# Which PSUM ring the small transposes of an attention kernel draw their banks from

## The chip, the cores and the metric

The kernel runs on one core of a Trainium2 chip. The metric is the device time of one execution in microseconds (us). The core's engines work side by side: PE (TensorE) multiplies and transposes matrices, DVE (VectorE), ACT (ScalarE) and POOL (GpSimd) work on elements, and queues, among them SP's (SyncE), issue DMAs. PEld in the profile is PE's loading of a stationary operand, which overlaps its matmuls. PE writes its results to PSUM, which this kernel uses as eight banks of 128 x 512 fp32; ACT and DVE read them from there.

## The reference

Three stages follow one another. The change lies in the first, an attention in which neighbouring pairs of queries are averaged:

```python
q_pool = q.reshape(B, H, S // factor, factor, D).mean(axis=3)
scores = scale * np.matmul(q_pool, k.transpose(0, 1, 3, 2))
scores = scores - np.max(scores, axis=-1, keepdims=True)
attn = np.exp(scores)
attn = attn / (np.sum(attn, axis=-1, keepdims=True) + 1e-09)
return np.matmul(attn, v).astype(np.float32)
```

There are 2 batches, 8 heads, 1152 keys, 576 pooled queries per batch, head size 64. Its 1152 x 512 output goes through a mixture of eight experts (two per row, 512 to 1024 to 512 with a relu), and then through a product with a 512 x 2048 matrix, `h * cos(h)`, and a product back to 512 columns. All is fp32; the kernel splits operands into a high and a low part in fp32r.

## The kernel before

**Tiles.** The attention takes the heads in four pairs (`hp`, 0 to 3; `hl` is the head in the pair). The pooled queries of both batches lie behind one another, 1152 rows, in nine tiles of 128 rows; tile 4 holds rows of both batches. So there are 72 tiles, numbered n = 18 hp + 9 hl + t. The scores of one tile are 128 x 1152, in three pieces of 384 columns, one PSUM bank each.

**One step.** The loop at line 880 is software-pipelined. In step n, PE makes the scores of tile n + 1 (`s_bank`, `s_part`, line 310) and transposes the exponentials p of tile n (`t_pe`, line 348); DVE takes the maxima of tile n + 1 (`s_max`, lines 324 and 326); ACT copies the transposed p as the high part (`t_hi`, line 361), makes the exponentials of tile n + 1 (`s_exp`, line 333), and copies the third piece of p for POOL (`t_pool`, lines 369 to 372); DVE makes the low part (`t_lo`, line 365). Then PE multiplies by the values (`avq`, line 386), nine products of a high and low part in some steps and six in the tiles 2 to 4 (`NPOP`), four of them ahead of the third transposes. The order on PE in one step is: scores 0 and 1, transposes 0, scores 2, transposes 1, four value products, transposes 2, the other value products, and last, in some steps, one small group.

**The small groups.** There are three kinds, each with a PSUM bank of its own for a short time:

- `q_group` (line 129): three transposes of pooled queries of the next head pair (line 136), then two ACT copies (line 140).
- `k_group` (line 174): three transposes of keys of the next head pair (line 180), then one ACT copy (line 181). Each of the two batches' key sets of a head pair takes three.
- `x_group` (line 684): for a row group of two or three tiles whose two heads are done, the products with an identity and the gate's weights (line 694), then two DVE multiplications by 1/sum (lines 706 and 723). In head pair 3, row group 1, ACT copies the bank first (line 698).

`plan()` (line 728) puts the first two kinds into fixed steps; the third goes into the next steps without one of these. In step 70, the last of the loop, the product of head pair 3, row group 1 is issued ahead of all transposes of p.

**PSUM.** The eight banks are three rings of one pool. Each name is a ring whose banks are handed out in turn, and a matmul into a bank waits until the readers of its last contents are done:

```python
def tbank():
    if tail:
        return ps.tile([128, 512], F32, name="s", bufs=4)
    return ps.tile([128, 512], F32, name="pt", bufs=3)
```

`s`, four banks, is for scores; `pt`, three banks, for the transposes of p and, through `tbank()`, for all small groups until the attention's tail; `pa`, one bank, for the value products. Three scores, three transposes and at most one small group are allocated in a step.

The order on every engine is the order of the code; nothing is rearranged. Behind the attention come routing, the experts and the last products (from line 949 on), whose weights DMAs load as buffers come free.

Of the kernel before, what the change touches and what calls it, by code (L numbers as in the profile page):

```python
# [9 lines left out]
F32 = mybir.dt.float32  # L10
# [12 lines left out]
def attn_moe_cos_kernel(ctx, tc, q, k, v, w_gate, w_noise, noise, w1, w2, w_in, w_out, out):  # L23
# [5 lines left out]
    HP = H // 2  # L29
# [35 lines left out]
    ps = pse.enter_context(tc.tile_pool(name="attps", bufs=1, space=PSUM))  # L65
# [56 lines left out]
# [4 lines that stand above are left out]
# [3 lines left out]
    def q_group(hp, j):  # L129
        if j == 0:  # L130
            QS[hp] = prep.tile([128, 1216], F32, name="st", bufs=1)
            nc.gpsimd.memset(QS[hp][:, SQ:QB1], 0.0)
        QR = QS[hp]
        p = tbank()
        for i in range(3):
            nc.tensor.transpose(p[:, i * 128:(i + 1) * 128], QP[hp][:, 3 * j + i].rearrange("p h d -> p (h d)"), ident)
        pv = p[:, 0:384].rearrange("p (i b s) -> p b s i", i=3, b=2)
        for b in range(B):
            o = QR[:, b * QB1:b * QB1 + SQ].rearrange("p (s c) -> p s c", c=9)[:, :, 3 * j:3 * j + 3]
            nc.scalar.activation(o, pv[:, b], AF.Copy, scale=1.0 / 16.0)  # L140
# [33 lines left out]
    def k_group(hp, b, j):  # L174
        if j == 0:
            KS[hp, b] = prep.tile([128, 1216], F32, name="st", bufs=1)[:, 0:S]
        p = tbank()
        for i in range(3):
            c = 128 * (3 * j + i)
            nc.tensor.transpose(p[:, i * 128:(i + 1) * 128], KN[hp, b].rearrange("p h s -> p (h s)")[:, c:c + 128], ident)  # L180
        nc.scalar.activation(KS[hp, b][:, 384 * j:384 * (j + 1)], p[:, 0:384], AF.Copy)
# [213 lines left out]
    def fold_x():  # L395
        hp, hl, g, p, w = fold.pop(0)
        b, lo, hi = GR[g]
        if g == 0:
            XT[hp, hl] = sb.tile([128, N], F32, name="xt", bufs=2)
        if (hp, hl) == (HP - 1, 1) and g > 1:  # L400
            nc.scalar.activation(XT[hp, hl][:, lo:hi], p[:, 0:w], AF.Copy)
        else:
            nc.vector.tensor_copy(XT[hp, hl][:, lo:hi], p[:, 0:w])
        if hl == 1:
            fill.append(lambda mid=None: x_group(hp, g, mid))
# [64 lines left out]
    def logits(hp, ts):  # L470
        acc = LGP[:, ts, 0:2]
        if hp == HP - 1:
            nc.vector.tensor_reduce(LG[:, ts], LGP[:, ts, 0:4].rearrange("p t h e -> p t e h"), axis=AX.X, op=OP.add)
        elif hp:
            nc.gpsimd.tensor_tensor(acc, acc, LGP[:, ts, 2 * hp:2 * hp + 2], op=OP.add)
# [208 lines left out]
    def x_group(hp, g, mid=None):  # L684
        tl = XTL[g]
        nt = len(tl)
        p = tbank()
        for i, t in enumerate(tl):
            if mid and i:
                mid()  # L690
                mid = None
            for hl in range(2):
                c = 160 * i + 80 * hl
                nc.tensor.matmul(p[:, c:c + 80], XT[hp, hl][:, t * 128:(t + 1) * 128],  # L694
                                 GW[:, hp, 16 * hl:16 * hl + 80], start=True, stop=True)
        if (hp, g) == (HP - 1, 1):
            xo = sb.tile([128, 3, 128], F32, name="rw", bufs=2).rearrange("p a b -> p (a b)")
            nc.scalar.activation(xo[:, 0:160 * nt], p[:, 0:160 * nt], AF.Copy)
            p = xo
        pv = p[:, 0:160 * nt].rearrange("p (i k c) -> p i k c", k=10, c=16)  # L700
        hs = slice(2 * hp, 2 * hp + 2)
        ts = slice(tl[0], tl[0] + nt)
        ri = RINV[:, ts, hs]

        def x_logits():
            nc.vector.tensor_tensor(LGP[:, ts, LGS[hp]:LGS[hp] + 2, :],
                                    pv[:, :, 0:10:9],
                                    ri.to_broadcast([128, nt, 2, 16]), op=OP.mult)
            logits(hp, ts)

        x_mul = lambda: x_store(hp, ts, pv[:, :, 1:9].rearrange("p i k c -> p i (k c)"), ri)
        if hp == HP - 1 and g:
            xm.append(x_mul)
            xg.append(x_logits)
        else:
            x_logits()
            x_mul()
# [3 lines left out]
    def x_store(hp, ts, px, ri):  # L721
        xo = X[:, ts, hp * 128:(hp + 1) * 128]
        nc.vector.tensor_tensor(xo.rearrange("p i (h d) -> p i h d", h=2),
                                px.rearrange("p i (h d) -> p i h d", h=2),
                                ri.to_broadcast([128, px.shape[1], 2, 64]), op=OP.mult)
        nc.sync.dma_start(x_d.rearrange("(t p) d -> p t d", p=128)[:, ts, hp * 128:(hp + 1) * 128], xo)

    def plan():
# [5 lines left out]
        for hp in range(HP):  # L734
# [6 lines left out]
            if hp:  # L741
                m = n0 - 18
                if hp > 1:
                    at(m, load_q, hp, 0)
                    at(m + 1, load_q, hp, 1)
                d = 1 if hp == 1 else 0
                at(m + 1 + d, pool_q, hp, 0)
                at(m + 2 + d, pool_q, hp, 1)
                at(m + 2, load_k, hp, 0)
                for j in range(3):  # L750
                    at(m + (3 + 2 * d, 5 + d, 6 + d)[j], q_group, hp, j)
                at(m + 7 + d, q_split, hp)
                at(m + 8 + d, q_asm, hp, 0)
                at(m + 9 + d, q_asm, hp, 1, False)
                for j in range(3):
                    at(m + (8 + d, 9 + d, 10 + d)[j], k_group, hp, 0, j)
                at(m + 11 + d, k_split, hp, 0)
                at(m + 11 + d, load_k, hp, 1)
                at(m + 12 + d, k_asm, hp, 0)
                for j in range(3):  # L760
                    at(m + (14, 15, 16)[j], k_group, hp, 1, j)
                at(m + 17, k_split, hp, 1)
                at(m + 18, k_asm, hp, 1)
                at(n0 + 1, l_asm, hp, 1)
                at(n0 + 1, q_bd, hp, 1)
# [60 lines left out]
    for j in range(3):  # L826
        k_group(0, 1, j)
# [52 lines left out]
    for n in range(NTOT - 1):  # L880
        hp, hl, t = tiles[n]
        for f, a in ev.get(n, []):
            if f not in (q_group, k_group):
                f(*a)
# [53 lines left out]
        if t in GEND:  # L938
            av_push(hp, hl, GEND[t])
            if hl == 1:  # L940
                r_inv(hp, GEND[t])
        fl = [(f, a) for f, a in ev.get(n, []) if f in (q_group, k_group)]
        for f, a in fl:
            f(*a)
# [430 lines left out]
    for e in range(E_N):  # L1375
        last = e == E_N - 1
        for f in range(8):
            s = 8 * e + f
# [334 lines left out]
```

## Time and profile before

| | us |
|---|---|
| median of three runs | 740.85 (740.27 to 741.19) |
| profiled execution | 739.14 |
| its span, first to last instruction | 737.6 |
| PE busy in the span | 722.5 |
| PE's weight loads busy | 673.9 |
| DVE, ACT, POOL busy | 562.3, 528.8, 301.9 |
| attention loop, steps 0 to 70 | about 14 to 270 in the span |

The page gives the busy time of each engine, the chain of work that ended last, and the costliest groups of instructions. "Timeline" lists instructions in order of time; a row may merge neighbours of one kind ("x3" is three of them, and the length is theirs together). "Waits" says who waited for whom; a wait is counted as idle time of the waiting engine. In brackets at the end of a row stands the idle time before it and what ended it. Names such as `s`, `pt` and `p` are the program's tiles: `p<-s,nm` is an exponential that reads the bank s. An ACTIVATE of line 333 is followed by a short read of its sum, which overlaps the next instruction.

### The profile page before, as it was taken

To read this page: it belongs to the slowest core of one execution; us is meant where nothing else is said; L and a number is where in the kernel's file an instruction comes from. 1 tells how busy PE (TensorE), PEld (TensorE's weight loads), DVE (VectorE), ACT (ScalarE), POOL (GpSimd) and SP (SyncE) were. 2 spreads that over 40 slices of the span, in tenths; PEclk is the share of its full clock that TensorE was granted. 3 is DMA by queue.
4 is the path that set the end of the run, shared out by engine and by line. 5 is a ranking of instruction groups with operands and counts; after the bars stand their busy time and mean duration, and the time that the engine had idled before them with its cause. 6 is when DMAs were issued, how large, how long until landed. Compare 5 with 4: busy or idle time off the path is not lost.

```text
span 737.6 us, 13760 instructions
## 1 busy us (share of the span) xinstructions
PE 722.5 (98%) x4803; PEld 673.9 (91%) x4803; DVE 562.3 (76%) x1161; ACT 528.8 (72%) x1200; POOL 301.9 (41%) x329
## 2 busy tenths in 40 slices
PE   6999999999999999999999999999999999999997
PEld 4899999999999989999999999999889989888885
DVE  5888788888878988879889887776677776556562
ACT  5999799979988964458777676766588665555443
POOL 5988867877977973212022021103187110000000
PEclk9999999999999999999999999999999999999999
DMA  9957756695665511798999999968353210010001
GB/s 207 244 94 183 184 130 147 163 237 106 161 140 146 179 44 29 248 314 295 363 371 328 334 345 330 329 233 286 119 171 97 85 29 1 1 44 0 1 1 60
DMA packets 75329, 125.02 MB, mean 169 GB/s; under 512 B 11950, under 2 KB 42030, under 8 KB 75254
## 3 DMA queue, kind: packets, MB, share of 16 engines
q1 hardware_dynamic: 68678, 101.92, 47.3%
q0 software_dynamic: 5568, 19.14, 7.4%
q10 hardware_dynamic: 1008, 3.02, 1.6%
q8 instruction: 40, 0.66, 0.4%
q14 instruction: 35, 0.29, 0.1%
HBM read 82.15 MB, written 20.33 MB: 139 GB/s over the span
## 4 chain that ended last, share of the span: by engine, by line
PE 90%; DVE 4%; ACT 3%; DMA 1%; issue 0%; SPq 0%; ACTq 0%; DVEq 0%
PE h L1145 20%; PE acc L1145 16%; PE acc L1177 11%; PE s L310 10%; PE pa L386 9%; PE pt L348 9%; PE t L1145 7%; PE pt L694 2%; PE t L1137 1%; PE pt L984 1%; PE t L1194 1%; PE pt L180 1%; DMA raw<-in_moe_w_dram 1%; DVE nm L324 1%; DVE el L365 1%; DMA qn<-in_q_dram 1%
## 5 line engine op out<-in xcount | busy, mean ns | idle before, releaser
L324 DVE TENSOR_REDUCE nm<-s 128x1 f32<-128x384 f32 x216 | 112.1, 551 | 23.4 <-PE s L310 21.8
L333 ACT ACTIVATE p<-s,nm 128x384 f32<-128x384 f32 x216 | 125.1, 583 | 2.8 <-DVE nm L326 1.5
L1145 PE MATMUL h<-xe,u 128*128 128x320 f32 (+5 forms) x768 | 120.1, 306 | 0.0
L1145 PEld LDWEIGHTS h<-xe,u 128*128 128x128 f32 x768 | 109.6, 188 | 0.5
L642 DVE TENSOR_TENSOR u<-raw,u 128x1024 fp32r<-128x1024 f32 x66 | 80.9, 1227 | 34.4 <-ACT u L641 33.6
L348 PE MATMUL pt<-ident,p 128*128 128x128 f32 x645 | 105.0, 272 | 0.0
L310 PE MATMUL s<-kt,q 128*128 128x384 f32 x240 | 88.8, 386 | 3.7 <-DVE kt L195 2.1
L348 PEld LDWEIGHTS pt<-ident,p 128*128 128x128 f32 x645 | 81.7, 140 | 5.7
L386 PE MATMUL pa<-eh,v 128*128 128x320 f32 (+1 forms) x279 | 86.5, 324 | 0.0
L641 ACT ACTIVATE u<-raw 128x1024 fp32r<-128x1024 f32 x73 | 77.1, 1057 | 10.3 <-DMA raw<-in_moe_w_dram 5.8
L361 ACT ACTIVATE eh<-pt 128x384 fp32r<-128x384 f32 x144 | 68.9, 501 | 20.3 <-PE pt L348 19.0
L386 PE MATMUL pa<-el,v 128*128 128x320 f32 (+1 forms) x279 | 82.4, 309 | 0.0
L372 POOL TENSOR_TENSOR el<-rw,eh 128x384 fp32r<-128x384 f32 x71 | 71.9, 1012 | 5.9
L365 DVE TENSOR_TENSOR el<-pt,eh 128x384 fp32r<-128x384 f32 x144 | 72.9, 547 | 1.0 <-ACT eh L361 0.9
L1177 PE MATMUL acc<-hh,u 128*128 128x320 f32 (+5 forms) x448 | 71.8, 302 | 0.1
L1145 PE MATMUL acc<-u,gh 128*128 128x512 f32 x216 | 66.9, 391 | 0.0
L310 PE MATMUL s<-kt,l 128*128 128x384 f32 x198 | 66.3, 337 | 0.0
L1177 PEld LDWEIGHTS acc<-hh,u 128*128 128x128 f32 x448 | 64.7, 188 | 0.4 <-ACT hh L1156 0.4
L1232 POOL DMA_DIRECT2D w_d<-dw x16 | 9.0, 563 | 130.5 <-DVE dw L1231 130.5
L371 POOL TENSOR_SCALAR eh<-rw 128x384 fp32r<-128x384 f32 x71 | 36.8, 518 | 42.0 <-ACT rw L369 39.7
L386 PEld LDWEIGHTS pa<-el,v 128*128 128x128 f32 x279 | 52.9, 190 | 0.0
L386 PEld LDWEIGHTS pa<-eh,v 128*128 128x128 f32 x279 | 52.8, 189 | 0.0
(292 smaller groups left out, 1605.9 us busy)
## 6 DMA issues: line engine op xcount, KB each, us to landing
raw<-in_moe_w_dram SPq DMA_DIRECT2D x64, 512.0 KB
raw<-in_moe_w_in_dram SPq DMA_DIRECT2D x16, 512.0 KB
raw<-in_moe_w_out_dram SPq DMA_DIRECT2D x16, 512.0 KB
w_d<-dw POOLq DMA_DIRECT2D x16, 512.0 KB, 5.4
raw<-w_d SPq DMA_DIRECT2D x13, 512.0 KB
vn<-in_v_dram SPq DMA_DIRECT2D x16, 288.0 KB
q<-sh SPq DMA_DIRECT2D x14, 304.0 KB
l<-ql SPq DMA_DIRECT2D x14, 304.0 KB
```

The costliest lines, as they stand in the source:

```text
L310: nc.tensor.matmul(o, l, r, start=(m == 0), stop=(m == len(mm) - 1))
L324: nc.vector.tensor_reduce(NM[n][:, i:i + 1], SB[n][i][:, 0:384], axis=AX.X, op=OP.max, negate=True)
L333: nc.scalar.activation(P[n][i], SB[n][i][:, 0:384], AF.Exp, bias=NM[n][:, 3:4], accum_out=SUMS[:, t, 2 * hp + hl, i:i + 1])
L348: nc.tensor.transpose(p[:, c], P[n][j][:, c], ident)
L361: nc.scalar.activation(t_dst(n, j)[0], t_src(n, j), AF.Copy)
L365: nc.vector.tensor_tensor(el, t_src(n, j), ef, op=OP.subtract)
L372: nc.gpsimd.tensor_tensor(el, rw, ef, op=OP.subtract)
L386: nc.tensor.matmul(st["p"][:, 0:w], V2[hp, hl, b][:, VC[c] if hp + b else c, :], (EH, EL)[s][:, c, EB[g]:EB[g] + w], start=(c == 0 and s = ...
L641: nc.scalar.activation(b[:, 0], r, AF.Copy)
L642: st_w["lo"].tensor_tensor(b[:, 1], r, b.bitcast(F32)[:, 0], op=OP.subtract)
L1145: nc.tensor.matmul(o, l, r, start=first and i == 0, stop=last and i == len(seq) - 1)
L1177: nc.tensor.matmul(ACC[e, d][:, 0:CAPS[e]], w[:, i, 128 * d:128 * d + 128], r[:, 0:CAPS[e]], start=f == 0 and r is hh and i == 0, stop=f = ...
```

## The change

Six of nine q groups (head pairs 2 and 3), eighteen of 21 key groups (head pairs 1 to 3) and fourteen products of row groups (all but the last two, which are in the tail and draw from `s` already) take their bank from the ring `s`. The ring's size, the code's order and all operations stay.

```diff
--- before.py
+++ after.py
@@ -131,7 +131,7 @@
             QS[hp] = prep.tile([128, 1216], F32, name="st", bufs=1)
             nc.gpsimd.memset(QS[hp][:, SQ:QB1], 0.0)
         QR = QS[hp]
-        p = tbank()
+        p = ps.tile([128, 512], F32, name="s", bufs=4) if hp > 1 else tbank()
         for i in range(3):
             nc.tensor.transpose(p[:, i * 128:(i + 1) * 128], QP[hp][:, 3 * j + i].rearrange("p h d -> p (h d)"), ident)
         pv = p[:, 0:384].rearrange("p (i b s) -> p b s i", i=3, b=2)
@@ -174,7 +174,7 @@
     def k_group(hp, b, j):
         if j == 0:
             KS[hp, b] = prep.tile([128, 1216], F32, name="st", bufs=1)[:, 0:S]
-        p = tbank()
+        p = ps.tile([128, 512], F32, name="s", bufs=4) if hp else tbank()
         for i in range(3):
             c = 128 * (3 * j + i)
             nc.tensor.transpose(p[:, i * 128:(i + 1) * 128], KN[hp, b].rearrange("p h s -> p (h s)")[:, c:c + 128], ident)
@@ -684,7 +684,7 @@
     def x_group(hp, g, mid=None):
         tl = XTL[g]
         nt = len(tl)
-        p = tbank()
+        p = ps.tile([128, 512], F32, name="s", bufs=4) if (hp, g) < (HP - 1, 2) else tbank()
         for i, t in enumerate(tl):
             if mid and i:
                 mid()
```

On PE, the place of the second key group of head pair 2 and the first two scores behind it. `kn` is the tile of keys, `kt`, `q` and `l` hold keys and the parts of q, `p` the exponentials; a row without a bracket waits for nothing new. Before:

```order
L180 MATMUL pt<-ident,kn 128x128 [waits DVE_49,PE_49]
L180 MATMUL pt<-ident,kn 128x128 [waits DMAHW0_49]
L180 MATMUL pt<-ident,kn 128x128
L310 MATMUL s<-kt,q_873 128x384
L310 MATMUL s<-kt,l_1422 128x384
L310 MATMUL s<-kt,q_873 128x384 [waits Activation_49]
L310 MATMUL s<-kt,l_1422 128x384
L348 MATMUL pt<-ident,p 128x128 [waits DVE_49]
L348 MATMUL pt<-ident,p 128x128 x2
L310 MATMUL s<-kt,q_873 128x384 [waits Activation_49]
L310 MATMUL s<-kt,l_1422 128x384
L348 MATMUL pt<-ident,p 128x128 [waits Activation_49]
```

With the change:

```order
L180 MATMUL s<-ident,kn 128x128 [waits Activation_49]
L180 MATMUL s<-ident,kn 128x128 [waits DMAHW0_49]
L180 MATMUL s<-ident,kn 128x128
L310 MATMUL s<-kt,q_873 128x384 [waits Activation_49]
L310 MATMUL s<-kt,l_1422 128x384
L310 MATMUL s<-kt,q_873 128x384 [waits Activation_49]
L310 MATMUL s<-kt,l_1422 128x384
L348 MATMUL pt<-ident,p 128x128 [waits DVE_49,PE_49]
L348 MATMUL pt<-ident,p 128x128 x2
L310 MATMUL s<-kt,q_873 128x384 [waits Activation_49]
L310 MATMUL s<-kt,l_1422 128x384
L348 MATMUL pt<-ident,p 128x128 [waits DVE_49]
```

The group's first transpose no longer waits for DVE but for ACT, the first score behind it has a wait for ACT that it did not have, and the transposes of line 348 wait for DVE where the second of them waited for ACT. The second and the third score wait for ACT in both, now for the readers of a bank that was filled one place later.

On PE, the scores of the last tile and the product of head pair 3, row group 1, behind them (`xt` is the attention's output by columns, `GW` the identity and the gate's weights). Before:

```order
L310 MATMUL s<-kt,q_2978 128x384
L310 MATMUL s<-kt,l_3576 128x384
L310 MATMUL s<-kt,q_2978 128x384 [waits Activation_49]
L310 MATMUL s<-kt,l_3576 128x384
L310 MATMUL s<-kt,q_2978 128x384 [waits Activation_49]
L310 MATMUL s<-kt,l_3576 128x384
L694 MATMUL pt<-GW,xt 128x80 [waits DVE_49,PE_49]
L694 MATMUL pt<-GW,xt 128x80 [waits DVE_49]
L694 MATMUL pt<-GW,xt 128x80 x2
L348 MATMUL pt<-ident,p 128x128 [waits PE_49]
```

With the change:

```order
L310 MATMUL s<-kt,q_2978 128x384 [waits DVE_49,PE_49]
L310 MATMUL s<-kt,l_3576 128x384
L310 MATMUL s<-kt,q_2978 128x384 [waits Activation_49]
L310 MATMUL s<-kt,l_3576 128x384
L310 MATMUL s<-kt,q_2978 128x384 [waits Activation_49]
L310 MATMUL s<-kt,l_3576 128x384
L694 MATMUL s<-GW,xt 128x80 [waits Activation_49]
L694 MATMUL s<-GW,xt 128x80 [waits DVE_49]
L694 MATMUL s<-GW,xt 128x80 x2
L348 MATMUL pt<-ident,p 128x128 [waits PE_49]
```

The first score has a wait for DVE, which leaves the bank of the product before it, and the product at line 694 waits for ACT.

## Rows read from the trace of the kernel before

**Rows 1.** Page, busy time, share of the span and instructions of each engine.

```profile
PE 722.5 (98%) x4803; PEld 673.9 (91%) x4803; DVE 562.3 (76%) x1161; ACT 528.8 (72%) x1200; POOL 301.9 (41%) x329
```

**Rows 2.** Table by stretches: stretch, busy us of PE, PEld, DVE, ACT, POOL, clock, DMA.

```profile
20.00:270.00 250.00, 248.23 (x1836) 237.46 (x1835) 210.11 (x511) 225.86 (x673) 199.38 (x223) 1.00 0.64 157
...
320.00:500.00 180.00, 179.87 (x1335) 178.97 (x1334) 150.53 (x207) 128.50 (x202) 30.77 (x35) 1.00 0.93 321
```

**Rows 3.** Waits of PE's loads, 20 to 270 us: total us, times, longest.

```profile
PEld s L310 <- ACT p L333: 5.2, 18, 1.0
PEld pt L694 <- PE pt L348: 1.0, 3, 0.3
```

**Rows 4.** Timeline, 115.3 to 118.8 us: start, length, engine, line, operation.

```profile
115.33 0.19 PEld L310 LDWEIGHTS s<-kt,q 128*128 128x128 f32 x1
...
115.92 0.59 ACT L333 ACTIVATE p<-s,nm 128x384 f32<-128x384 f32 x1
...
115.98 1.58 DVE L324 TENSOR_REDUCE nm<-s 128x1 f32<-128x384 f32 x3 [0.73 <-PE s L310]
...
116.35 0.19 PEld L310 LDWEIGHTS s<-kt,q 128*128 128x128 f32 x1
...
116.64 0.42 PEld L348 LDWEIGHTS pt<-ident,p 128*128 128x128 f32 x3
...
116.81 0.49 PE L348 MATMUL pt<-ident,p 128*128 128x128 f32 x3
116.85 0.98 ACT L361 ACTIVATE eh<-pt 128x384 fp32r<-128x384 f32 x2
...
117.60 0.16 DVE L326 TENSOR_REDUCE nm<-nm 128x1 f32<-128x3 f32 x1
...
117.86 0.58 ACT L333 ACTIVATE p<-s,nm 128x384 f32<-128x384 f32 x1
...
118.76 0.19 PEld L310 LDWEIGHTS s<-kt,q 128*128 128x128 f32 x1
```

**Rows 5.** Timeline, 121.3 to 122.1 us.

```profile
121.31 0.58 ACT L333 ACTIVATE p<-s,nm 128x384 f32<-128x384 f32 x1
...
122.03 0.32 PEld L310 LDWEIGHTS s<-kt,q 128*128 128x128 f32 x2
```

**Rows 6.** Timeline, first key group of a second set.

```profile
66.87 0.59 ACT L333 ACTIVATE p<-s,nm 128x384 f32<-128x384 f32 x1
...
67.36 0.19 PEld L310 LDWEIGHTS s<-kt,q 128*128 128x128 f32 x1
```

**Rows 7.** Timeline, first q group of head pair 2.

```profile
95.28 0.59 ACT L333 ACTIVATE p<-s,nm 128x384 f32<-128x384 f32 x1
...
95.57 0.19 PEld L310 LDWEIGHTS s<-kt,q 128*128 128x128 f32 x1
```

**Rows 8.** Timeline, a step with nine value products.

```profile
74.06 0.59 ACT L333 ACTIVATE p<-s,nm 128x384 f32<-128x384 f32 x1
...
74.74 0.19 PEld L310 LDWEIGHTS s<-kt,q 128*128 128x128 f32 x1
```

**Rows 9.** Timeline, the last product of a row group in the loop.

```profile
264.65 0.59 ACT L333 ACTIVATE p<-s,nm 128x384 f32<-128x384 f32 x1
...
264.72 1.04 PEld L694 LDWEIGHTS pt<-GW,xt 128*128 128x128 f32 x8
...
266.03 0.44 ACT L698 ACTIVATE rw<-pt 128x320 f32<-128x320 f32 x1 [0.70 <-PE pt L694]
```

**Rows 10.** Timeline, PE's loads, a product of three row tiles.

```profile
85.34 0.30 PEld L694 LDWEIGHTS pt<-GW,xt 128*128 128x128 f32 x2 [0.20 <-issue]
```

**Rows 11.** Waits of ACT, 20 to 270 us.

```profile
ACT eh L361 <- PE pt L348: 19.0, 50, 1.5
```

## The prediction

> **What bounds the kernel now.** I read the page's busy times first: PE, the matrix engine, is busy 98% of the span and no other engine passes 76% [rows 1]. A modelled PE time can hide idle time, so the second view is the table by stretches: in the attention loop, 20 to 270 us, the weight loads alone fill 237.46 of 250 us, at a granted clock of 1.00, and from 320 to 500 us they fill 178.97 of 180 us [rows 2]. So PE bounds the loop and what follows it, and a wait put before a PE instruction in the loop moves the end by its whole length, unless the loop's own slack takes it.
>
> The third view is what PE's loads wait for in the loop [rows 3]. The ring of four banks named s already runs dry now and then: 18 waits of a score load for ACT's exponential, 5.2 us in all. The ring of three named pt shows three waits of a row group's product, 1.0 us in all. There is no row at all for a transpose of p (line 348) waiting. The change takes customers out of the second ring and puts them into the first.
>
> The last view is the timeline of single steps, [rows 4] and on. The reader should look at two engines together there: when ACT ends the third exponential of a tile, and when PE loads the third score of the next tile.
>
> **What the change removes, adds and moves.** No instruction is added, dropped or reordered, on any queue; only the banks change, and with them who waits for whom. Thirty-eight groups move: six of q (head pairs 2 and 3), eighteen of keys (head pairs 1 to 3), fourteen products of row groups. A ring hands its banks out in fixed turn, so an allocation waits for the readers of the one four places before it. A step takes three s banks: the third score of a tile waits for the second exponential of the tile before. With a group between two tiles, each of the next three scores waits for a release one place later, and the third score waits for the third exponential, the last thing but one that ACT does in a step.
>
> What a release costs: the second score of a tile waits for the first exponential in [rows 5]; that ends at 121.31 + 0.58 = 121.89 and the load starts at 122.03, so 0.14 us from ACT's end to PE's load. These are the waits of which [rows 3] count 18. I use 0.14 in every term: the needed time is the exponential's end + 0.14, and what the load starts earlier than that now is the new wait.
>
> Key groups in front of steps with six value products, six places [rows 4]: the exponential ends at 115.92 + 0.59 = 116.51, needed 116.65, the load starts at 116.35: 0.30 each, **1.80 us**. Does it reach ACT? The transpose behind that score is loaded at 116.64 and ends at 116.81 + 0.49 = 117.30; ACT's second copy starts half way through the pair at 116.85, about 117.34. Moved by 0.30, the transpose ends at 117.60 and the copy is about 0.26 late, and with it the exponential at 117.86. The maxima on DVE, done at 117.60, that this exponential also needs follow the same score. So ACT, which has no gap there, is late too, and nothing is won back.
>
> First key group of a second set, three places [rows 6]: 66.87 + 0.59 + 0.14 = 67.60 against 67.36: 0.24 each, **0.72 us**.
>
> First q group of head pairs 2 and 3, two places [rows 7]: 95.28 + 0.59 + 0.14 = 96.01 against 95.57: 0.44 each, **0.88 us**. The tile there crosses the two batches, and PE comes early.
>
> Key and q groups in front of steps with nine value products, twelve places [rows 8], and the one key group left, which I cost like these: 74.06 + 0.59 + 0.14 = 74.79 against 74.74: 0.05 each, 13 x 0.05 = **0.65 us**.
>
> Products of row groups inside the loop, thirteen places: PE is long at the product and DVE and ACT are ahead, so the next scores wait for nothing. I cost them at nothing; the cover is the product itself, about the 1.04 us of the load row in [rows 9], and without it they would cost 0.05 like the others, 0.65. The last of them (head pair 3, second row group) is different. It is issued right behind the last tile's scores, so it needs the bank of the third score of the tile before: 264.65 + 0.59 + 0.14 = 265.38, and its load starts at 264.72 [rows 9]. That is **0.66 us**. ACT already waits 0.70 us for this product [rows 9], and the transposes of the tile stand behind it on PE, so it goes to the end in full.
>
> What is taken away: the three waits of [rows 3], 1.0 us, and 0.20 us before the product of three row tiles at 85.34 [rows 10], which waits in the same way: **1.2 us**. The group there no longer waits for DVE to leave a pt bank.
>
> Sum: 1.80 + 0.72 + 0.88 + 0.65 + 0.66 = 4.71; less 1.2 is **+3.5 us**. Copies, reductions, POOL's splits and all DMAs keep their place and length: they read the same columns from another bank. They come later only by what PE loses, and the splits feed scores a whole head later.
>
> The unknown cost is the hand-over. Were a release seen at once, the terms would be 6 x 0.16, 3 x 0.10, 2 x 0.30, nothing and 0.52, or 2.38, and the net +1.2. At the other end what is freed goes straight into the next wait, as a product that comes earlier meets a score that may not: nothing won, +4.7, and rounded up by the smaller waits of a second score in front of a third, +5.0. I keep +3.5, because 0.14 is measured on the same two engines and the same pair of lines.
>
> The Trainium skill has a figure for this, in "Advanced Engine Details and Errata", section Network/Comms: a sequencer reads a semaphore in 50 to 100 ns. With 0.05 and 0.10 in place of 0.14 the sum would be about +1.8 and +2.5 (estimates from that page). The row's 0.14 lies above its range, and the row decides.
>
> **The sum against the times.** The durations come from the profiled execution, 739.14 us with a span of 737.6; with the change it would take 742.6. The median of the three runs shown is 740.85, 1.7 above it, and the same +3.5 gives **744.3 us**, 0.5% longer. A measurement of this kernel can tell about 0.2%, 1.5 us, from no change.
>
> **The rivals.** *The delay stays on PE.* If ACT runs at its own pace in the six places of [rows 4] and the two of [rows 7], PE catches up behind it and 1.80 + 0.88 drop out: 4.71 - 2.68 - 1.2 = +0.8, or 741.6 us. For it: ACT has no gap in [rows 4] and its step of 118.76 - 115.33 = 3.43 us is longer than the products need. Against it: the transposes that ACT copies stand behind the delayed score. Chance 0.14.
>
> *Faster: the free ring feeds ACT.* ACT waits 19.0 us in 50 places for transposes of p [rows 11], 0.38 us each. If these wait for a pt bank that a group held, a ring of its own lets them start early, and ACT with them. A third of them, 17 x 0.38 = 6.4, against +3.5 gives -2.9, or 737.9 us. It decides from 13 of them on: 13 x 0.38 = 5.0, the +3.5 and the 1.5 that can be told. Against it: the load of a transpose follows the score's with no gap in [rows 4], and [rows 3] have no wait of line 348. ACT simply is at the copy before PE is. Chance 0.09.
>
> *The clock falls.* PE now stops for a moment in most steps. In the loop it has stopped 18 times for a score already, and the granted clock stayed at 1.00 of 2.4 GHz [rows 2, 3], so I give this 0.03. If one block of three steps ran at 1.2 GHz, each step of 3.43 us would take twice that, +10.3 and with the +3.5 about 754.7 us. The Trainium skill names such a case in "TensorE: Matmul & The Clock Gate", section "A second HAM failure mode: psum-queue depth-cycling", where short stops between matmul groups as banks turn over make the clock swing between its two levels; by that rule the change would do it, and the rows of before show the stops without the fall.
>
> That the change does not do what it says can be left aside: PE's order shows every group's new bank and its new waits.
>
> **How the numbers follow.** Forecast 0.74, with a range of its own from +1.2 to +5.0, that is 742.1 to 745.9; the delay stays on PE 0.14; faster 0.09; the clock 0.03. Slower by over 0.2% takes all of the forecast but its lowest end, and the clock: 0.71 + 0.03 = 0.74. Within 0.2% is the first rival and that end: 0.14 + 0.03 = 0.17. Faster is 0.09. The range goes down to the first rival with a microsecond for its own error, 740.6, and up to 746.2, just over the forecast's own; it leaves out the faster rival, the clock and a few hundredths of the rest.
>
> **What would show it.** In the profile after, PE's loads of a score waiting for ACT's exponential should go from 18 waits and 5.2 us to some 40 waits and 8 to 10 us, and the waits of the row groups' product before a transpose should be gone. The step at 115.33 should be 3.7 us long in place of 3.43, and the loop should end 3 to 4 us later, with the stretch behind it as long as before. The last product should start right behind ACT's third exponential and not before it. I am wrong if the waits of scores grow by less than 2 us, if they grow and the loop ends no later, or if ACT's 19.0 us of waits for transposes shrink by more than 3 us.

## The result and the profile after

The change made the kernel slower: 743.52 us (median of 7 runs, 742.29 to 746.52) against 740.51 (7 runs, 738.09 to 741.36). The ratio is 1.0054, with an interval of 1.0034 to 1.0074, or +4.0 us (2.5 to 5.5); it is not the quotient of the two medians, which are 3.0 us apart. The forecast was +3.5, a ratio of 1.0047.

The busy times on the page of the changed kernel do not show where the loss is [rows 1]: the same instructions on every engine and the same shares for PE and its loads. PE's busy time, whose ends are modelled, grew by 6.1 us with the span, and that of its loads by 1.8.

```profile
PE 728.6 (98%) x4803; PEld 675.7 (91%) x4803; DVE 562.1 (76%) x1161; ACT 529.3 (71%) x1200; POOL 303.8 (41%) x329
```

The waits of PE's loads in the loop, 20 to 275 us (the end is 5 us later than in [rows 3], since the loop is):

```profile
PEld s L310 <- ACT p L333: 9.2, 33, 1.6
PEld s L694 <- ACT p L333: 0.6, 1, 0.6
```

Scores wait 33 times and 9.2 us in place of 18 times and 5.2 us, and the waits of a row group's product for a pt bank are gone. A new row has come: one product waits for ACT's exponential, 0.6 us. The two rows are the whole answer: the view lists nothing else that PE's loads wait for there.

Two things limit this view. It leaves out waits shorter than 0.15 us, and its stretch begins ahead of the changed part, where the two executions differ as well. From the first score of tile 10 on, scores wait 14 times and 2.9 us before, and 28 times and 6.1 us after. Of the 14 new waits, eleven are those of a third score, in the tiles 11, 12, 29, 30, 47, 48, then 16, 34, 52, then 23 and 41: the six, three and two places to which the prediction gave 0.24 us or more. In the kernel before, no third score waits there. The other three are the second scores of the tiles 23 and 41 and the first score of tile 13.

The same view for ACT:

```profile
ACT eh L361 <- PE pt L348: 22.4, 62, 1.6
ACT p L333 <- DVE nm L326: 2.3, 8, 0.7
```

ACT's waits for the transposes have not shrunk from the 19.0 of [rows 11]; they have grown to 22.4.

The timeline of the step that answers to [rows 4], PE's loads and ACT, with DVE's first maximum:

```profile
118.54 0.19 PEld L310 LDWEIGHTS s<-kt,q 128*128 128x128 f32 x1
...
119.14 0.59 ACT L333 ACTIVATE p<-s,nm 128x384 f32<-128x384 f32 x1
...
119.88 0.19 PEld L310 LDWEIGHTS s<-kt,q 128*128 128x128 f32 x1 [0.23 <-ACT p L333]
...
120.53 0.56 DVE L324 TENSOR_REDUCE nm<-s 128x1 f32<-128x384 f32 x1 [0.30 <-PE s L310]
...
120.86 0.49 ACT L361 ACTIVATE eh<-pt 128x384 fp32r<-128x384 f32 x1 [0.27 <-PE pt L348]
...
121.37 0.58 ACT L333 ACTIVATE p<-s,nm 128x384 f32<-128x384 f32 x1
...
122.28 0.19 PEld L310 LDWEIGHTS s<-kt,q 128*128 128x128 f32 x1
```

Read it from the top. ACT's third exponential ends at 119.14 + 0.59 = 119.73. The third score of the next tile is loaded 0.15 behind that, where before it was loaded 0.16 ahead of the same event. DVE's third maximum then waits 0.30 for the score, and ACT's second copy waits 0.27 for the transposes behind it; before, ACT went through both copies without a gap. The step takes 122.28 - 118.54 = 3.74 us in place of 3.43.

**Where the time lies.** The two profiled executions are 5.8 us apart in span, 743.4 against 737.6, which is more than the runs differ. So the span is taken apart. The load of the first score of tile 10 and that of tile 71 bound the part of the loop with the moved groups. On PE's timeline, before:

```profile
46.10 0.19 PEld L310 LDWEIGHTS s<-kt,q 128*128 128x128 f32 x1
...
263.43 0.19 PEld L310 LDWEIGHTS s<-kt,q 128*128 128x128 f32 x1
```

and after:

```profile
48.41 0.19 PEld L310 LDWEIGHTS s<-kt,q 128*128 128x128 f32 x1
...
268.30 0.19 PEld L310 LDWEIGHTS s<-kt,q 128*128 128x128 f32 x1
```

That part grew from 217.33 to 219.89 us, **+2.6**. From tile 71's first score to the last load for the transposes of that tile's p it is 6.09 and 6.69, **+0.6**. From there to the experts nothing changed (0.03 us). These are the +3.1 us that the change made in this execution. The rest lies elsewhere: 2.3 us had been lost ahead of tile 10, where the two programs are the same; the stretch from the experts' first product to the end of ACT's last copy took 446.10 us in place of 444.94, and what follows it, the last output DMAs, 3.98 in place of 4.82. The first of these differs as much between executions of kernels that leave it alone; for the second that is less sure (last section).

The last product, which answers to [rows 9]:

```profile
269.52 0.59 ACT L333 ACTIVATE p<-s,nm 128x384 f32<-128x384 f32 x1
...
270.25 0.97 PEld L694 LDWEIGHTS s<-GW,xt 128*128 128x128 f32 x8 [0.65 <-ACT p L333]
...
271.49 0.44 ACT L698 ACTIVATE rw<-s 128x320 f32<-128x320 f32 x1 [1.29 <-PE s L694]
```

It is loaded 0.14 behind the exponential's end at 270.11 and has waited 0.65 for it; ACT's copy of it waits 1.29 where it waited 0.70.

The product of three row tiles that waited 0.20 in [rows 10] follows PE's value product without a gap:

```profile
88.23 0.19 PEld L386 LDWEIGHTS pa<-el,v 128*128 128x128 f32 x1
88.36 1.42 PEld L694 LDWEIGHTS s<-GW,xt 128*128 128x128 f32 x12
```

The table by stretches, in the columns of [rows 2]:

```profile
20.00:270.00 250.00, 248.27 (x1805) 233.69 (x1804) 207.88 (x506) 223.86 (x665) 195.95 (x218) 1.00 0.65 158
320.00:500.00 180.00, 179.76 (x1332) 178.32 (x1332) 148.90 (x206) 126.14 (x199) 33.27 (x34) 1.00 0.94 325
```

PE's loads fill 233.69 of the loop's 250 us where they filled 237.46; the granted clock is 1.00 in both stretches.

### The profile page after: what moved, and what is told of

Its sections match the earlier page's. It is cut to its first block, busy times and chain, and to the rows that moved or that the text cites. A ratio compares the mean times of both kernels' runs of the same rounds, so it can differ in the third digit from the quotient of the medians.

```text
span 743.4 us, 13764 instructions
## 1 busy us (share of the span) xinstructions
PE 728.6 (98%) x4803; PEld 675.7 (91%) x4803; DVE 562.1 (76%) x1161; ACT 529.3 (71%) x1200; POOL 303.8 (41%) x329
## 4 chain that ended last, share of the span: by engine, by line
PE 87%; DMA 4%; DVE 4%; ACT 3%; issue 1%; POOL 0%; SPq 0%; ACTq 0%; DVEq 0%; POOLq 0%
PE h L1145 18%; PE acc L1145 14%; PE s L310 11%; PE acc L1177 11%; PE pa L386 9%; PE pt L348 9%; PE t L1145 7%; PE s L694 2%; DMA qn<-in_q_dram 1%; PE pt L984 1%; DMA raw<-in_moe_w_dram 1%; PE t L1194 1%; PE t L1137 1%; DMA raw<-in_moe_w_out_dram 1%; DMA raw<-w_d 1%
## 5 line engine op out<-in xcount | busy, mean ns | idle before, releaser
L310 PEld LDWEIGHTS s<-kt,q 128*128 128x128 f32 x240 | 43.8, 189 | 13.8 <-ACT p L333 9.2
```

Source lines behind the costliest of these rows:

```text
L310: nc.tensor.matmul(o, l, r, start=(m == 0), stop=(m == len(mm) - 1))
```

## The experiments

The theory and the rivals are those of the prediction. All runs were compared with the kernel before on the same chip; its median was 739.73 us in the first four and 739.61 in the others. "Loop" is the part from tile 10's to tile 71's first score load, against the 217.3 us of before.

| kernel | median us | ratio and interval | loop | last tile to last transposes |
|---|---|---|---|---|
| e1_keys | 742.92 | 1.0048 (1.0030 to 1.0065) | +2.69 | -0.01 |
| e2_q | 740.45 | 1.0013 (1.0002 to 1.0023) | +0.88 | 0.00 |
| e3_rows | 738.57 | 0.9986 (0.9974 to 0.9998) | -1.33 | -0.01 |
| e4_after_swap | 740.16 | 1.0000 (0.9991 to 1.0010) | -0.90 | +0.20 |
| e5_before_swap | 740.75 | 1.0011 (0.9998 to 1.0023) | -0.07 | -0.01 |
| e7_no_last | 742.81 | 1.0037 (1.0025 to 1.0050) | +2.60 | -0.01 |
| e8_no_last_swap | 739.23 | 0.9994 (0.9984 to 1.0003) | -0.85 | 0.00 |
| e9_rows_swap | 738.98 | 0.9983 (0.9971 to 0.9994) | -1.49 | -0.01 |

### e1_keys: only the keys' groups move

In `k_group` alone, of the kernel before:

```diff
-        p = tbank()
+        p = ps.tile([128, 512], F32, name="s", bufs=4) if hp else tbank()
```

> Only the 18 key groups draw from s; q groups and products of row groups stay in pt. Theory (each group makes the next tile's third score wait for the third exponential of the tile before, and the wait is passed on whole): the terms of the keys, 6 x 0.30 + 3 x 0.24 + 9 x 0.05 = +3.0 us by the start of the last tile's scores, and nothing given back at the row groups: ratio about 1.004, slower than the full change at that point. Rival (every moved group costs about the same, 3.2 us over 38 groups, 0.085 each): 18 x 0.085 = +1.5 us. Rival (the delay stays on PE): +1.2 us at most.

The loop is 2.69 us longer, near the theory's +3.0 and far from the +1.5 and +1.2 of the rivals. The waits of PE's loads, 20 to 275 us:

```profile
PEld s L310 <- ACT p L333: 8.0, 27, 1.9
PEld pt L694 <- PE pt L348: 1.0, 3, 0.3
```

The keys make the larger part of the change's loss, and the three waits of the row groups' products stay, since their banks still come from pt. But the product of three row tiles that waited 0.20 in [rows 10] does not wait here, though its bank is a pt bank, too:

```profile
87.63 0.19 PEld L386 LDWEIGHTS pa<-el,v 128*128 128x128 f32 x1
87.82 1.41 PEld L694 LDWEIGHTS pt<-GW,xt 128*128 128x128 f32 x12
```

Its load starts 0.11 to 0.12 us behind the end of DVE's low part (line 365) in all four kernels that leave it in pt. But ACT's copies, which DVE follows, scatter there: the first starts 1.98 to 2.17 us behind the tile's first score in these four. So the product waits 0.20 before, 0.14 in e2, 0.05 in e5 and not at all here. That is scatter between executions, and up to 0.2 us of it is in every difference to the loop of before. Without that one step the keys cost +2.9.

### e2_q: only q's groups move

The same line in `q_group`, with `if hp > 1`.

> Only the 6 q groups of head pairs 2 and 3 draw from s. Theory: 2 x 0.44 + 4 x 0.05 = +1.1 us by the start of the last tile's scores, in two jumps of about 0.5 at the tile that crosses the batches (steps from tile 23 to 24 and from 41 to 42). Rival (every moved group costs 0.085): +0.5 us, spread over six steps.

The loop is 0.88 us longer. Step by step it is two jumps, 0.47 between the first scores of tiles 23 and 24 and 0.48 between those of tiles 41 and 42: the first q group of head pairs 2 and 3, as reckoned (0.44 each). The first of them on PE's timeline, behind the group:

```profile
95.53 0.35 PEld L136 LDWEIGHTS s<-ident,qp 128*128 128x128 f32 x3
96.03 0.19 PEld L310 LDWEIGHTS s<-kt,q 128*128 128x128 f32 x1
...
96.59 0.19 PEld L310 LDWEIGHTS s<-kt,q 128*128 128x128 f32 x1 [0.27 <-ACT p L333]
```

Here the second score waits, too. These are the scores of tile 23, the tile right behind the one that crosses the batches.

### e3_rows: only the row groups' products move, without the last

In `x_group` alone; the last product (head pair 3, row group 1) stays in pt:

```diff
-        p = tbank()
+        p = ps.tile([128, 512], F32, name="s", bufs=4) if (hp, g) < (HP - 1, 1) else tbank()
```

> Only the 13 products of row groups inside the loop draw from s; keys, q groups and the product of head pair 3, row group 1 stay in pt. Theory: these cost nothing and give back the waits before the products of the third and fourth row group, 0.26 + 3 x 0.35 to 0.41 = -1.2 to -1.4 us by the start of the last tile's scores: ratio about 0.998, faster than before and than the change. Rival (every moved group costs 0.085): +1.1 us. Rival (what is freed is eaten by the next wait): 0.

The loop is 1.33 us shorter, in four steps of 0.26 to 0.40, at the three products of [rows 3] and the one of [rows 10]; and this kernel is faster than the one before, by 0.14% with an interval of 0.02 to 0.26%, and so than the changed one. The waits of scores did not move by a tenth of a microsecond:

```profile
PEld s L310 <- ACT p L333: 5.2, 18, 1.0
```

So moving these groups costs nothing and gives back what they waited. Three of the four steps are firm, 1.05 us together; the fourth, 0.26 at the product of [rows 10], is up to 0.2 us the scatter of the one execution that it is compared with (e1). That the product's own length is what covers the new waits fits this, but no run varied it. The loss lies in the other two kinds and the last product. Leaving out the step of [rows 10], the three parts add up: +2.89 for the keys, +0.94 for q and -1.07 for the row groups make +2.76, and the full change has +2.83.

### e4_after_swap: the full change, with the third exponential one copy earlier

In the step of the changed kernel, ACT's third exponential goes ahead of its copy for POOL:

```diff
-        t_pool(n, 2)
         s_exp(n + 1, 2)
+        t_pool(n, 2)
```

> The full change, with two ACT instructions of a step exchanged: the third exponential now goes ahead of the copy of the third transposes (0.37 us from start to start in the profile of before). Theory: the third exponential ends 0.37 us earlier, so the waits of the third score vanish (0.05 and 0.24 and 0.30 are below 0.37; 0.44 leaves 0.07), the last product's 0.66 falls to 0.29, and what is left are the second scores' waits for the second exponential, 0.10 in six places, 0.05 in three and 0.23 in two, 1.2 us; with the 1.3 given back, +0.1 to +0.3 us against before, some 3 us less than the full change. Rival (the waits come from the groups' own readers or from bank traffic in general, not from that exponential): the same +3.2 as the full change. Rival (the copy that POOL needs is now too late): a new wait of the value products for POOL, slower than the full change.

If the waits come from where the third exponential stands in ACT's order, making it earlier must take them away with the banks left as the change has them. In the exchange it starts 0.56 us behind the second exponential in place of 0.93, so 0.37 us earlier. It does take them away: the loop falls from +2.57 to -0.90 us, between the first scores of the tiles 10 and 71 at

```profile
46.16 0.19 PEld L310 LDWEIGHTS s<-kt,q 128*128 128x128 f32 x1
...
262.57 0.19 PEld L310 LDWEIGHTS s<-kt,q 128*128 128x128 f32 x1
```

and the waits of scores fall from 33 and 9.2 to

```profile
PEld s L310 <- ACT p L333: 5.9, 21, 1.0
```

The loop came out 0.8 lower than I expected. I had left some 1.2 us for the second scores, whose release the exchange does not move. The step that answers to [rows 4] shows why much of that is missing:

```profile
114.72 0.57 ACT L333 ACTIVATE p<-s,nm 128x384 f32<-128x384 f32 x1
...
115.28 0.58 ACT L333 ACTIVATE p<-s,nm 128x384 f32<-128x384 f32 x1
```

on ACT, and on PE

```profile
115.06 0.19 PEld L310 LDWEIGHTS s<-kt,q 128*128 128x128 f32 x1
...
115.44 0.19 PEld L310 LDWEIGHTS s<-kt,q 128*128 128x128 f32 x1
115.55 0.19 PEld L310 LDWEIGHTS s<-kt,l 128*128 128x128 f32 x1
...
116.12 0.19 PEld L310 LDWEIGHTS s<-kt,q 128*128 128x128 f32 x1
...
118.52 0.19 PEld L310 LDWEIGHTS s<-kt,q 128*128 128x128 f32 x1
```

The second score is loaded 0.15 after its exponential's end at 115.29 and 0.38 after the first score. In the kernel before it was 0.28, from 115.33 in [rows 4] to

```profile
115.61 0.19 PEld L310 LDWEIGHTS s<-kt,q 128*128 128x128 f32 x1
115.79 0.19 PEld L310 LDWEIGHTS s<-kt,l 128*128 128x128 f32 x1
```

The first of the second score's two loads comes 0.10 later, but its other load only 0.03 later: 115.55 - 115.06 = 0.49 against 115.79 - 115.33 = 0.46. Before, PE's loads stood 0.18 apart there, now 0.11. So PE had most of this tenth to spare between the two loads, and the delay ends there. The third score comes 0.26 after the end of the third exponential, without a wait, and the step takes 3.46 us, 0.03 more than before.

Outside the loop the exchange costs: the last product still waits 0.27 and puts the last transposes off by 0.20, and behind them the tail to its own product of a row group is 0.73 longer. There ACT's copy of the third piece of p, POOL's split of it and PE's value product stand behind the exponential now; that they are what lengthens it is read from the order and was not tested. With the loop that sums to about nothing, and the ratio is 1.0000.

### e5_before_swap: the exchange in the kernel before

The edit of e4, without the change.

> The kernel before with the two ACT instructions exchanged in every step, as in e4_after_swap, as its control. Theory: in the kernel before no load waits for the third exponential, so the exchange gives nothing in the loop (0.0 us to within 0.1 at the start of the last tile's scores). Rival (what the exchange won in e4 came from somewhere else than the waits on that exponential, say from POOL or the transposes): the loop is 2 to 3 us shorter here too. In the last step, where the exchange makes POOL's copy later by about 0.6 us, the attention's tail is expected to be up to 0.7 us longer.

The first scores of the tiles 10 and 71 are loaded at

```profile
46.33 0.19 PEld L310 LDWEIGHTS s<-kt,q 128*128 128x128 f32 x1
...
263.57 0.19 PEld L310 LDWEIGHTS s<-kt,q 128*128 128x128 f32 x1
```

so the loop does not move (-0.07), and the exchange by itself wins nothing there: what e4 took away in the loop is the change's own loss. The tail is 0.56 us longer.

### e7_no_last: the full change without the last product

```diff
-        p = ps.tile([128, 512], F32, name="s", bufs=4) if (hp, g) < (HP - 1, 2) else tbank()
+        p = ps.tile([128, 512], F32, name="s", bufs=4) if (hp, g) < (HP - 1, 1) else tbank()
```

> The full change, but the product of head pair 3, row group 1 stays in pt. Theory: the loop is as with the full change, +2.6 us from step 10 to the start of the last tile's scores, and the 0.66 us wait before the product and its copies is gone: +2.6 us at the last transposes in place of +3.2, ratio about 1.0035. Rival (that wait is hidden by ACT and DVE behind it): the distance from the last tile's first score to the last transposes is the same as with the full change.

From the last tile to the last transposes it takes as long as before, while the loop stays at +2.60. The 0.6 us is the last product's alone.

### e8_no_last_swap and e9_rows_swap: both repairs together

To spare the tail, the exchange is left out in the last step; e8 adds it to e7, e9 to e3:

```diff
+        if n < NTOT - 2:
+            s_exp(n + 1, 2)
         t_pool(n, 2)
-        s_exp(n + 1, 2)
+        if n == NTOT - 2:
+            s_exp(n + 1, 2)
```

> As e7_no_last, and the third exponential ahead of the copy for POOL in every step but the last. Theory: the waits of the third scores are gone but for 0.2 at the two batch-crossing tiles, the row groups' 1.3 us stay won, and without the exchange in the last step the tail does not pay for it: -0.8 to -0.9 us against before, ratio about 0.999, 3.5 us less than e7_no_last. Rival (the tail pays whatever the last step does): 0.

> Only the 13 products of row groups inside the loop in s, as e3_rows, with the exchange in every step but the last. Theory: with keys and q groups in pt no load waits for the third exponential, so the exchange adds nothing to the -1.2 us of e3_rows: -1.2 to -1.4, ratio 0.998. Rival (the exchange frees something of its own): more than 2 us.

Both loops came out near what was expected, -0.85 and -1.49, the second 0.1 beyond its range. The time did not follow in full: the tail is 0.27 and 0.28 us longer, although its last step has the old order. In e8 ACT's waits for transposes fell below those of [rows 11], yet in the loop it is no faster than the row groups' products alone make it (20 to 275 us):

```profile
ACT eh L361 <- PE pt L348: 17.2, 49, 1.3
```

What lengthens the tail there was not settled. e9 is faster than the kernel before, by 0.06 to 0.29%, but cannot be told from e3, which is the simpler edit.

## Why the prediction was right

**The path.** The prediction's chain was: the bank's release one place later, PE's third score late, the transposes behind it late, ACT's copy and the next exponential late, the step longer. Every link stands in the step shown: 0.15 after the exponential's end, ACT's copy 0.27 late (reckoned 0.26), 3.74 us (reckoned 3.7). e4 shows the cause and not only the company: with the banks as in the change and the release 0.37 us earlier, the loss is gone, and e5 shows that the exchange wins nothing without the change.

**The terms.** The steps' own shifts, taken from the load of one tile's first score to that of the next, before against after:

| term | places | forecast us | measured us |
|---|---|---|---|
| key groups, [rows 4] and its like | 6 | +1.80 | +1.72 (0.26 to 0.30 each) |
| first key group of a second set | 3 | +0.72 | +0.73 |
| first q group of a head pair | 2 | +0.88 | +0.96 |
| other key and q groups | 13 | +0.65 | +0.57 |
| given back at four products | 4 | -1.20 | -1.29 |
| all other steps of the loop | 33 | 0 | -0.12 |
| last product | 1 | +0.66 | +0.59 |
| sum | | +3.5 | +3.1 in the profile; +4.0 (2.5 to 5.5) in the runs |

The loop's six lines make the +2.57. The interval of the runs, 2.5 to 5.5, holds the forecast and the profile's +3.1 alike, so it is the terms that bear the prediction out and not the closeness of +3.5.

The hand-over was the price that carried all of it. I had 0.14 from [rows 5], and it is 0.13 to 0.14 at every one of the 18 waits before and the 34 after, taken from the trace's unrounded times. The Trainium skill's 50 to 100 ns for a semaphore's read ("Advanced Engine Details and Errata", section Network/Comms) would have made the sum an estimated +1.8 to +2.5; the row was the better guide.

The thirteen small places were the least certain: 0.05 each is the difference of two larger times, and it came out at 0.03 to 0.05, with one of 0.12 (tile 13, whose first score waits). The cost of nothing for the row groups' products inside the loop is what e3 shows. The 0.20 of [rows 10] was right for that execution but is no steady term: in e1 the same wait was not there.

Two labels in the working are wrong and change no term. The six places of [rows 4] are not all in front of steps with six value products: the step shown, with tile 29, has nine, and so have those with tiles 11 and 47. What the six share is the step ahead of the group, with nine value products of 256 columns. And the scores that wait in [rows 7] are those of tile 23, behind the tile that crosses the batches.

**The counts.** I looked for some 40 waits of scores and found 33, since a wait of 0.05 is too short for the view. The 9.2 us are inside the 8 to 10 that I gave, but 0.8 of the growth lies ahead of tile 10 and is not of the change. The stretch behind the loop was as long as before up to the experts; behind that it was 1.2 us longer in the profile, up to ACT's last copy, which I had not looked for. e3 and e7 have it too, and e4 does not, though it draws the same banks as the change; whether the change has a part in it stays open (last section).

**The rivals.** *The delay stays on PE*: in the changed kernel it does not, ACT waits 0.27 in the step that I had taken for it. Nor is it a matter of size: at the small places delays of 0.03 to 0.05 reach the next step, too, and the tenth that does stay on PE, in e4, is taken up between the two loads of one score. *The free ring feeds ACT*: ACT's waits for transposes grew by 3.4 us in place of shrinking, and e3, which frees pt at the row groups' products alone, has a loop that is shorter by about the waits of these products and no more. *The clock falls*: the granted clock stayed at 1.00 of 2.4 GHz in the loop and from 320 to 500 us, with 33 stops for a score in the loop. The case in the Trainium skill by which such stops would have been costly ("TensorE: Matmul & The Clock Gate", section "A second HAM failure mode: psum-queue depth-cycling") did not show here.

## What to carry to other kernels

In this kernel a ring of banks had no slack of its own. What an allocation waits for is the reader of the one that lies a ring's length before it, so write down, for each place of a new customer, which reader that becomes and when it ends. Move only those behind which nothing waits anew, which here were the row groups' products (0.14% faster), and look at the last step by itself, where nothing follows that could win a delay back. Where a ring runs dry, what matters is the place of the releasing instruction in its engine's order: 0.37 us earlier took away the 2.6 us that the loop had lost.

## What the runs showed of the hardware

The hand-over from the end of ACT's exponential to PE's load into the bank hardly varies: 0.13 to 0.14 us at all 52 waits of the two kernels, from 20 to 275 us.

Two stretches whose code no edit touched differ between executions. The first score of tile 10 was loaded between 46.10 and 48.41 us, before any bank is drawn otherwise. Part of this comes with the inputs: POOL's additions of the pooled queries at line 211 wait for an input DMA; on the timeline, before:

```profile
12.13 2.78 POOL L211 TENSOR_TENSOR qp<-qn 64x576 f32<-64x576 f32 x2 [1.83 <-DMA qn<-in_q_dram]
```

and after:

```profile
13.12 2.77 POOL L211 TENSOR_TENSOR qp<-qn 64x576 f32<-64x576 f32 x2 [2.42 <-DMA qn<-in_q_dram]
```

Here 1.0 of the 2.3 us are there already. And the stretch from the experts' first product to the end of ACT's last copy took 444.7 to 445.0 us in seven of the ten profiled executions, and 445.9 to 446.1 in the three of the changed kernel, e3 and e7. These three are just the kernels that have row groups' products in s without the exchange, so with one profile of each it cannot be called chance. Against a cost of the banks speaks that e4, e9 and e8 draw the same ones as the changed kernel, e3 and e7, in this order, and take no longer than before, and that the medians of e3 and e7 differ from the kernel before by -1.2 and +3.2 us, with loops of -1.3 and +2.6. What makes it so was not looked into. A difference of one or two microseconds between two profiles of this kernel is therefore read by stretches that the edit touches, and not from the spans.
